# Weight sums for the seven-block back products made inside the second layer, in four of eight slice pairs

## The chip, the cores and the metric

The kernel runs on one core of a Trainium2 chip. The metric is the device time of one execution in microseconds (us), lower being better. A core has TensorE (PE, matmuls), VectorE (DVE), ScalarE (ACT), GpSimd (POOL) and SyncE (SP), which here only issues DMAs. Each engine works off its own queue in order; an instruction at the head of a queue that waits holds back everything behind it.

## What is computed

A circular convolution along the sequence (by FFT), then two gated layers on 6016 tokens with 256 channels. The change is in the second one, `_moe2_ref`.

```python
def reference(**kwargs):
    ...
    attn_out = _attn_ref(**attn_kwargs)      # irfft(rfft(x) * F), (2, 3008, 256)
    x = attn_out.reshape(B * S, D)
    x = _moe_ref(x=x, **moe_kwargs)          # (sigmoid(x @ w_gate) * (x @ w_val)) @ w_out
    return _moe2_ref(x=x, **moe2_kwargs)

def _moe2_ref(x, w_in, w_out):               # w_in (256, 2048), w_out (2048, 256)
    h = x @ w_in
    g = h * (1.0 / (1.0 + np.exp(-1.702 * h)))
    return (g @ w_out).astype(np.float32)
```

## The kernel before

**Numbers.** The weights arrive as 64-bit floats and are decoded on the chip into a high part `hi` and a low part `lo`, both stored as fp32r. A product is three matmuls (`mm3`, lines 126 to 128: hi*hi, hi*lo, lo*hi), here each 128 x 128 weights by 512 tokens (448 in the last round).

**Rounds.** The second layer takes the tokens as six rounds `p` = 0 to 5 of two tiles each (10 tiles of 512, 2 of 448). A round has eight iterations `fp` = 0 to 7, one per pair of 128-wide slices of the 2048 hidden units. An iteration makes the 2 x 2 blocks of hidden values z, y, w, x by seven forward products instead of eight (in program order x0, y4, x5, z1, x6, y2, x3), applies the gate, splits the result into high and low halves, and queues the back products (with `w_out`), which run as `back()` calls between the forward products of the next iteration: one after x0, one after y4, two after z1, two after y2, two after x3.

**Seven-block back products.** An ordinary iteration needs eight back products. In rounds 1 to 5 the iterations with `fp` in `SEVEN = (1, 3, 5)` use seven instead (class `Seven`, `backs()`: m1 to m7). That takes differences of the gate results (t1 to t4: `after_y`, `after_x`, then `third`, `fourth`, `fourth_low` in the next iteration), a bank `ps[3]` shared by m1, m6, m7 and m5, which `keep` (L1847, L1849) empties into `sums` on DVE after each of the four, and four weight sums. One of these sums takes the place of `wp(2 * fp, 1)` in the weight tile itself, three are in `sout` and are reloaded from the DRAM tensor `oscr` for each use (`load_sout`, L1785, L1786).

**Decoding.** The sixteen weight jobs `j` of the second layer (even: `w_in`, odd: `w_out` of slice pair `j // 2`) are decoded by `decode_chores`, a list of small steps that `spend` deals out between the products, from the end of the first layer (L146 loads, L221 to L247 decoding) into round 0. An even job also makes weight sums for the forward products (`sums`, `end`). An odd job of a slice pair in `SEVEN` makes its four back sums in the same steps from the unsplit value, puts the first sum's halves in the `c` buffer, and writes all four to `oscr` (L286, L287). `load_s1` (L1792) brings the first one into the weight tile later in round 0. The `c` buffer is single; L223 of the next job writes it.

**Order.** All engines follow the written order. In round 0, an iteration first runs all steps that its own slice pair still lacks, and only then issues products:

```python
                while 2 * fp + 1 not in done:
                    spend(chores, 1)
```

The same step list carries the splitting of the next round's inputs (`forms_chores`: four differences, then seven high/low splits; L1147, L1152, L1158 to L1170), appended in round 0 at `fp` = 6 at the latest.

Of the kernel before, what the change touches and what calls it, by code (L numbers as in the profile page):

```python
# [89 lines left out]
def kernel(  # L90
# [120 lines left out]
    def decode_chores(j, st, place):  # L211
# [48 lines left out]
        def sums(k):  # L260
# [7 lines left out]
            else:  # L268
                nc.vector.tensor_sub(r[:, 2], v[:, 0, 0], v[:, 0, 1])
                nc.vector.tensor_sub(r[:, 3], v[:, 1, 0], r[:, 1])  # L270
                if j % 2:
                    c = t["c"].bitcast(F32R)
                    t["s1"] = c[:, :P], c[:, P:2 * P]
                else:
                    t["s1"] = hi[:, P:2 * P], lo[:, P:2 * P]
                nc.scalar.activation(out=t["s1"][0], in_=r[:, 0], func=AF.Copy)
                nc.scalar.activation(out=sp[0], in_=r[:, 1:], func=AF.Copy)

        def end():
            r = t["r"]  # L280
# [2 lines left out]
            if j % 2:
                k = SEVEN.index(fp)
                for i in range(2):
                    nc.sync.dma_start(out=oscr[k, i, :, :P], in_=t["s1"][i].bitcast(F32))  # L286
                    nc.sync.dma_start(  # L287
                        out=oscr[k, i, :, P:], in_=sp[i].rearrange("p k m -> p (k m)").bitcast(F32)
                    )
                summed_out.add(fp)  # L290
            else:
                spill()
# [1489 lines left out]
    def load_sout(fp):  # L1782
        k = SEVEN.index(fp)
        for i in range(2):
            nc.sync.dma_start(out=wo[i][:, FC1 - 1, :].bitcast(F32), in_=oscr[k, i, :, P:3 * P])  # L1785
            nc.sync.dma_start(out=sx0[i][:, 5, :].bitcast(F32), in_=oscr[k, i, :, 3 * P:])  # L1786

    def load_s1(fp):
        assert fp in summed_out
        k = SEVEN.index(fp)  # L1790
# [263 lines left out]
```

## Time and profile before

| what | value |
|---|---|
| three timed runs | 1137.73, 1138.62, 1139.47 us (median 1138.62) |
| the profiled execution | 1139.96 us, of which the span is 1138.2 |
| granted TensorE clock, mean of the span | 0.995 |
| busy in the span: PE, DVE, ACT, POOL | 98%, 72%, 59%, 39% |

The span runs from the first to the last instruction; the 1.8 us beside it lie outside the instructions. A matmul's end is modelled, so successive matmuls overlap in the list, and the pitch from start to start tells what one costs. The second layer begins near 647 us: round 0 to 739.5, then five rounds of about 79.6 us (the last one shorter, with 448 tokens a tile).

### The profile page before, as it was taken

To read this page: it belongs to the slowest core of one execution; us is meant where nothing else is said; L and a number is where in the kernel's file an instruction comes from. 1 tells how busy PE (TensorE), PEld (TensorE's weight loads), DVE (VectorE), ACT (ScalarE), POOL (GpSimd) and SP (SyncE) were. 2 spreads that over 40 slices of the span, in tenths; PEclk is the share of its full clock that TensorE was granted. 3 is DMA by queue.
4 is the path that set the end of the run, shared out by engine and by line. 5 is a ranking of instruction groups with operands and counts; after the bars stand their busy time and mean duration, and the time that the engine had idled before them with its cause. 6 is when DMAs were issued, how large, how long until landed. Compare 5 with 4: busy or idle time off the path is not lost.

```text
span 1138.2 us, 15096 instructions
## 1 busy us (share of the span) xinstructions
PE 1119.7 (98%) x5027; PEld 900.1 (79%) x5027; DVE 814.7 (72%) x1369; ACT 668.3 (59%) x1272; POOL 439.6 (39%) x366
## 2 busy tenths in 40 slices
PE   9999999999999999999999998799999999999998
PEld 4378887677888888888888887588888888888897
DVE  6989998786688655878777787747657567477444
ACT  4655555554455545655655656556667657576665
POOL 3810004654333311211211123156566556566554
PEclk9999999999999999999999999899999999999999
DMA  8755238793200300126155262021030020200100
GB/s 203 202 180 181 93 122 224 188 187 81 79 1 1 109 1 1 51 87 131 46 181 186 65 224 75 5 88 29 1 102 15 19 84 15 71 27 15 51 29 32
DMA packets 95244, 99.09 MB, mean 87 GB/s; under 512 B 40320, under 2 KB 67200, under 8 KB 95168
## 3 DMA queue, kind: packets, MB, share of 16 engines
q1 hardware_dynamic: 93200, 95.24, 29.9%
q10 hardware_dynamic: 1968, 2.91, 0.8%
q8 instruction: 39, 0.64, 0.2%
q14 instruction: 37, 0.30, 0.1%
HBM read 61.81 MB, written 32.37 MB: 83 GB/s over the span
## 4 chain that ended last, share of the span: by engine, by line
PE 88%; DVE 4%; DMA 2%; ACT 1%; issue 1%; SPq 0%; POOL 0%; ACTq 0%; DVEq 0%; POOLq 0%
PE ps L126 29%; PE ps L128 29%; PE ps L127 29%; PE ps L344 2%; DVE yp L1152 1%; DMA oscr<-c 0%; DMA wg<-wscr 0%; DMA yraw<-tt 0%; DMA fi<-in_fd_dram 0%; DVE c L235 0%; DVE z L520 0%; DVE a L554 0%; DVE ps L1980 0%; DVE xs L1162 0%; DVE g L1751 0%
## 5 line engine op out<-in xcount | busy, mean ns | idle before, releaser
L1751 POOL TENSOR_TENSOR g<-sg,g 128x512 fp32r<-128x512 f32 (+1 forms) x90 | 122.0, 1360 | 153.1 <-ACT sg L1739 144.7
L123 POOL TENSOR_TENSOR g<-sg,g 128x512 fp32r<-128x512 f32 (+1 forms) x47 | 59.5, 1267 | 257.3 <-ACT g L122 257.3
L126 PE MATMUL ps<-yp,wg 128*128 128x512 f32 (+2 forms) x382 | 149.8, 393 | 0.0
L128 PE MATMUL ps<-yp,wg 128*128 128x512 f32 (+2 forms) x382 | 147.8, 387 | 0.0
L127 PE MATMUL ps<-yp,wg 128*128 128x512 f32 (+2 forms) x382 | 147.7, 387 | 0.0
L127 PE MATMUL ps<-g,wo 128*128 128x512 f32 (+2 forms) x303 | 116.6, 385 | 0.0
L126 PE MATMUL ps<-g,wo 128*128 128x512 f32 (+2 forms) x303 | 116.6, 386 | 0.0
L128 PE MATMUL ps<-g,wo 128*128 128x512 f32 (+2 forms) x303 | 116.5, 385 | 0.0
L1751 POOL TENSOR_TENSOR wo<-sg,wo 128x512 fp32r<-128x512 f32 (+1 forms) x57 | 78.9, 1387 | 53.9 <-ACT sg L1739 48.0
L126 PEld LDWEIGHTS ps<-yp,wg 128*128 128x128 f32 x382 | 71.7, 188 | 26.2 <-issue 13.0
L128 PEld LDWEIGHTS ps<-yp,wg 128*128 128x128 f32 x382 | 71.7, 188 | 14.3
L127 PEld LDWEIGHTS ps<-yp,wg 128*128 128x128 f32 x382 | 71.7, 188 | 13.1 <-issue 0.3
L1966 DVE TENSOR_TENSOR ps<-ps,tabs 128x512 f32<-128x512 f32 (+1 forms) x48 | 32.9, 686 | 61.6 <-PE ps L128 60.4
L1738 ACT ACTIVATE g<-ps 128x512 fp32r<-128x512 f32 (+1 forms) x70 | 41.3, 589 | 58.5 <-DVE ps L1968 55.6
L1649 ACT ACTIVATE sg<-ps 128x480 f32<-128x480 f32 (+1 forms) x48 | 28.1, 586 | 70.4 <-DVE ps L1647 70.4
L1683 DVE TENSOR_TENSOR g<-ps,g 128x480 fp32r<-128x480 f32 (+1 forms) x48 | 32.4, 675 | 48.6 <-ACT g L1680 48.4
L126 PEld LDWEIGHTS ps<-g,wo 128*128 128x128 f32 x303 | 56.9, 188 | 11.5 <-issue 0.8
L128 PEld LDWEIGHTS ps<-g,wo 128*128 128x128 f32 x303 | 56.9, 188 | 10.9
L127 PEld LDWEIGHTS ps<-g,wo 128*128 128x128 f32 x303 | 56.9, 188 | 10.8
L1739 ACT ACTIVATE sg<-ps 128x512 f32<-128x512 f32 (+1 forms) x107 | 62.9, 587 | 0.2 <-POOL g L1751 0.2
L1668 ACT ACTIVATE sg<-ps 128x480 f32<-128x480 f32 (+1 forms) x48 | 28.0, 584 | 39.8 <-PE ps L128 39.6
L1751 POOL TENSOR_TENSOR ks<-sg,ks 128x512 fp32r<-128x512 f32 (+1 forms) x30 | 39.5, 1316 | 28.9 <-ACT sg L1739 24.8
(371 smaller groups left out, 3138.1 us busy)
## 6 DMA issues: line engine op xcount, KB each, us to landing
yscr<-tt SPq DMA_DIRECT2D x56, 128.0 KB, 2.3
raw<-in_w_out_dram SPq DMA_DIRECT2D x14, 512.0 KB, 4.5
yraw<-xscr SPq DMA_DIRECT2D x14, 512.0 KB, 5.1
x<-in_xd_dram SPq DMA_DIRECT2D x32, 192.0 KB, 3.9
wscr<-wl SPq DMA_DIRECT2D x24, 256.0 KB, 2.0
wg<-wscr SPq DMA_DIRECT2D x24, 256.0 KB, 3.0
out_dram<-yraw SPq DMA_DIRECT2D x20, 256.0 KB, 2.2
f<-in_fd_dram SPq DMA_DIRECT2D x23, 192.0 KB, 4.2
```

Source lines behind the costliest of these rows:

```text
L123: lo_eng.tensor_sub(dst_lo, src, dst_hi.bitcast(F32))
L126: nc.tensor.matmul(out=o, lhsT=w[0], rhs=x[0], start=first, stop=False, **kw)
L127: nc.tensor.matmul(out=o, lhsT=w[0], rhs=x[1], start=False, stop=False, **kw)
L128: nc.tensor.matmul(out=o, lhsT=w[1], rhs=x[0], start=False, stop=last, **kw)
L344: nc.tensor.matmul(out=o[c], lhsT=w[64 * r:64 * r + n], rhs=x(r, k), start=True, stop=True, tile_position=(64 * r, 64 * k),)
L1649: nc.scalar.activation(out=sgz, in_=z, func=AF.Sigmoid)
L1668: nc.scalar.activation(out=sgy, in_=y, func=AF.Sigmoid)
L1683: nc.vector.tensor_sub(g0[1], x, g0[0].bitcast(F32))
L1738: nc.scalar.activation(out=self.gp[0], in_=self.bank, func=AF.Gelu_apprx_sigmoid)
L1739: nc.scalar.activation(out=self.sg, in_=self.bank, func=AF.Gelu_apprx_sigmoid)
L1751: eng.tensor_sub(self.gp[1], self.sg, self.gp[0].bitcast(F32))
L1966: nc.vector.tensor_add(y, x, s5[:, :n])
```

## The change

`SEVEN` becomes `(1, 2, 4, 5)`. An odd job's decoding makes no sums any more. New steps `out_sums` add the two halves of the stored weights, make the four sums from that, split them, and write one into the weight tile and three to `oscr`; they are dealt out from the last iteration of round 0 on, into round 1. `load_s1` is gone. In a slice pair that follows another seven-block one, `load_sout` fetches the three parts one at a time, each behind the back product that used it last. m3 goes ahead of m1, the seventh back product goes ahead of `after_x`, and the step rates change.

```diff
-    SEVEN = (1, 3, 5)
-    oscr = dram.tile([len(SEVEN), 2, P, 4 * P], F32, name="oscr")
+    SEVEN = (1, 2, 4, 5)
+    oscr = dram.tile([len(SEVEN), 2, P, 3 * P], F32, name="oscr")
...
-        sums_ = [lambda: sums(0), low, lambda: sums(1), end]
-        if j % 2:
-            sums_ = [low, sums_[0], sums_[2], end] if fp in SEVEN else [low]
-        return [start, mant, sign, value] + sums_
+        return [start, mant, sign, value] + ([low] if j % 2 else [lambda: sums(0), low, lambda: sums(1), end])
...
             if not q and bulk and not hold_back:
                 q.extend(next_decode(bulk.pop(0)))
+            elif not q and out_jobs:
+                q.extend(out_sums(out_jobs.pop(0)))
...
+    def load_sout(fp, *ks):
+        q = SEVEN.index(fp)
+        for k in ks:
+            for i in range(2):
+                nc.sync.dma_start(out=sout[k][i].bitcast(F32), in_=oscr[q, i, :, k * P:(k + 1) * P])
+
+    def out_sums(fp):
+        w = slot(2 * fp + 1)
+        q = SEVEN.index(fp)
+        one, two = ("ex", "c") if q % 2 == 0 else ("c", "ex")
+        t = {}
+
+        def whole():
+            t["v"] = st.tile([P, 512], F32, tag=one, name="wv")
+            nc.vector.tensor_add(t["v"], *[x.bitcast(F32) for x in w])
+
+        def sums():
+            v = t["v"].rearrange("p (c i m) -> p c i m", c=2, m=P)
+            r = t["r"] = st.tile([P, 4, P], F32, tag=two, name="wr")
+            nc.vector.tensor_add(r[:, 0], v[:, 0, 1], v[:, 1, 1])
+            nc.vector.tensor_sub(r[:, 1], r[:, 0], v[:, 0, 0])
+
+        def more():
+            v, r = t["v"].rearrange("p (c i m) -> p c i m", c=2, m=P), t["r"]
+            nc.vector.tensor_sub(r[:, 2], v[:, 0, 0], v[:, 0, 1])
+            nc.vector.tensor_sub(r[:, 3], v[:, 1, 0], r[:, 1])
+            t["hi"] = st.tile([P, 512], F32R, tag="m", name="wh")
+            nc.scalar.activation(out=t["hi"], in_=r.rearrange("p k m -> p (k m)"), func=AF.Copy)
+
+        def low():
+            lo = st.tile([P, 512], F32R, tag=one, name="wlo")
+            nc.vector.tensor_sub(lo, t["r"].rearrange("p k m -> p (k m)"), t["hi"].bitcast(F32))
+            for i, x in enumerate((t["hi"], lo)):
+                nc.sync.dma_start(out=oscr[q, i], in_=x[:, P:].bitcast(F32))
+                nc.sync.dma_start(out=w[i][:, P:2 * P].bitcast(F32), in_=x[:, :P].bitcast(F32))
...
-            return [m1, m3, m6, m2, m7, m4, m5]
+            return [m3, m1, m6, m2, m7, m4, m5]
...
             if p == 0:
+                if fp == LAST:
+                    out_jobs += SEVEN
...
-            if not asked and (fp >= 3 if p else fp >= 4 and not bulk and not chores or fp == 6):
+            if not asked and (fp >= (4 if p == 1 else 2) if p else fp >= 4 and not bulk and not chores or fp == 6):
...
-                rate = (3, 2, 0) if seven else (1, 1, 1) if was else (0, 2, 2) if fp == LAST else (2, 1, 1)
+                if seven:
+                    rate = (1 + (p == 1), 1 + (fp == 2 and p == 1), 0) if was else (3, 2, 0)
+                elif was:
+                    rate = (2, 2, 1) if p == 1 and fp > 3 else (1, 2, 1)
+                else:
+                    rate = (0, 2, 2) if fp == LAST else (2 + (p == 1), 2 + (p == 1), 2)
...
             if seven:
+                back()
                 seven.after_x()
```

Three places show what moves. The first is DVE at the end of round 0. Before, this is the last iteration (`fp` = 7): seven low halves and the last decode (L221 to L247) stand in one block ahead of its first sum (L1966).

```order
L1152 TENSOR_TENSOR xk_1644<-xs,xk_1643 128x512
L221 TENSOR_SCALAR ex<-raw 128x512
L225 TENSOR_SCALAR m<-raw 128x512
L229 SCALAR_TENSOR_TENSOR m<-raw,m 128x512
L235 SCALAR_TENSOR_TENSOR c<-raw,c 128x512
L241 SCALAR_TENSOR_TENSOR m<-m,c 128x512
L247 TENSOR_TENSOR wl_2831<-m,wl_2830 128x512
L1966 TENSOR_TENSOR ps_73<-ps_72,tabs 128x512
```

After, the last decode's final step (L247) stands in `fp` = 5, and the first differences of the next round's inputs follow it there.

```order
L247 TENSOR_TENSOR wl_2831<-m,wl_2830 128x512
L1736 TENSOR_TENSOR g_2871<-ps_73,g_2870 128x512
L1140 TENSOR_TENSOR xs<-yraw 128x512
L1144 TENSOR_TENSOR xs<-yraw,xs 128x512
L1148 TENSOR_TENSOR yraw<-yraw 128x512
L1990 TENSOR_TENSOR ps_73<-ps_71,tabs 128x512
```

The last decode has moved up by two iterations, and no block of steps stands ahead of the first sum of `fp` = 7.

The second place is round 1, iteration `fp` = 1, on DVE in the changed kernel: the sums of the third `out_sums` job (`wr<-wv`) stand between the iteration's second and third sum; the two DMA queues named in the wait are those of the copies that the second job issues from its low half. The SP queue behind them is shown below it, from the last output write (L1757) on.

```order
L1990 TENSOR_TENSOR ps_73<-ps_72,tabs 128x512 [waits PE_49,Activation_49]
L1992 TENSOR_TENSOR ps_71<-ps_71,s_2835 128x512 [waits PE_49]
L1786 TENSOR_TENSOR wr<-wv 128x128 [waits DMAHW4_49,DMAHW3_49,DVE_49]
L1787 TENSOR_TENSOR wr<-wr,wv 128x128 [waits DVE_49]
L1791 TENSOR_TENSOR wr<-wv 128x128
L1792 TENSOR_TENSOR wr<-wv,wr 128x128 [waits DVE_49]
L2006 TENSOR_TENSOR sg<-ps_72,tabs 128x512 [waits PE_49,Pool_49]
```

```order
L1757 DMA out_dram<-yraw 128x512 [waits DMAHW0_49,DVE_49]
L1771 DMA sx_1641<-oscr 128x128 [waits DMAHW1_49]
L1771 DMA sx_1642<-oscr 128x128 [waits DMAHW3_49,DMAHW2_49]
L1771 DMA wo_86<-oscr 128x128
L1771 DMA wo_87<-oscr 128x128 [waits DMAHW4_49]
L1771 DMA wo_86<-oscr 128x128 [waits DMAHW5_49]
L1771 DMA wo_87<-oscr 128x128 [waits DMAHW6_49]
L705 DMA yraw<-xscr 128x2x512 [waits DMAHW7_49]
L705 DMA yraw<-xscr 128x2x512 [waits DMAHW0_49]
L1800 DMA oscr<-wh 128x384 [waits DMAHW1_49]
L1801 DMA wg_84<-wh 128x128 [waits DMAHW2_49,PE_49]
L1800 DMA oscr<-wlo 128x384 [waits DMAHW3_49,DVE_49]
L1801 DMA wg_85<-wlo 128x128 [waits DMAHW4_49,PE_49]
```

Before, nothing stands between those two sums on DVE, and SP has no `oscr` writes in round 1.

The third place is round 2 on DVE, an iteration in which a seven-block pair's back products run. Before (`fp` = 2), from one first sum (L1966) to the next:

```order
L1966 TENSOR_TENSOR ps_73<-ps_71,tabs 128x512
L1968 TENSOR_TENSOR ps_72<-ps_72,s_2835 128x512
L1847 COPY sums<-ps_74 128x512
L1751 TENSOR_TENSOR g_2869<-spare,g_2868 128x512
L1980 TENSOR_TENSOR sg<-ps_71,tabs 128x512
L1847 COPY sums<-ps_74 128x512 x2
L1158 TENSOR_TENSOR xs<-yraw 128x512
L1162 TENSOR_TENSOR xs<-yraw,xs 128x512
L1166 TENSOR_TENSOR yraw<-yraw 128x512
```

After (`fp` = 2, whose own back products are seven too), from the third sum (L2006) on:

```order
L1144 TENSOR_TENSOR xs<-yraw,xs 128x512
L2006 TENSOR_TENSOR sg<-ps_71,tabs 128x512
L1864 COPY sums<-ps_74 128x512
L1823 TENSOR_TENSOR sg<-ps_73,sg 128x512
L1825 TENSOR_TENSOR spare<-sg,ps_73 128x512
L1829 TENSOR_TENSOR sg<-sg 128x512
L1864 COPY sums<-ps_74 128x512
L1736 TENSOR_TENSOR g_2869<-ps_71,g_2868 128x512
L1840 TENSOR_TENSOR spare<-ps_71,sg 128x512
L1148 TENSOR_TENSOR yraw<-yraw 128x512
L1866 TENSOR_TENSOR sums<-sums,ps_74 128x512
```

The differences of `after_y` and `after_x` (L1823 to L1840) now stand among the `keep` copies (L1864, L1866), in one iteration.

## Rows read from the trace of the kernel before

**Rows 1.** Waits of PE's matmuls, longest: engine line, released by, us, times, longest

```profile
PE ps L126 <- ACT s L1946: 8.3, 1, 8.3
PE ps L126 <- DVE wo L1751: 3.2, 1, 3.2
```

**Rows 2.** Windows: stretch, length, busy PE, PEld, DVE, ACT, POOL, clock, DMA, GB/s

```profile
680.00:690.00 10.00, 6.84 (x29) 5.36 (x28) 4.72 (x8) 5.06 (x10) 2.66 (x2) 0.97 0.51 171
690.00:700.00 10.00, 10.00 (x39) 8.12 (x39) 7.84 (x15) 5.70 (x13) 1.29 (x1) 0.86 0.18 60
720.00:730.00 10.00, 1.94 (x9) 1.28 (x7) 9.24 (x16) 4.38 (x9) 0.35 (x1) 0.85 0.00 1
730.00:740.00 10.00, 9.77 (x36) 7.95 (x37) 3.81 (x6) 4.84 (x10) 1.78 (x2) 0.81 0.01 2
...
820.00:900.00 80.00, 80.00 (x355) 66.24 (x354) 50.30 (x73) 53.00 (x99) 48.53 (x36) 1.00 0.13 42
```

**Rows 3.** Chain that ended last, 678 to 688 us: start, us, what

```profile
678.89 5.64 DMA oscr<-c
...
687.34 0.70 DVE wo L1751
```

**Rows 4.** The same chain, 717 to 730 us

```profile
717.16 1.75 DVE xs L1158
...
729.71 0.48 ACT s L1946
```

**Rows 5.** Timeline of PE: start us, us, line, operation, shape; [idle before]

```profile
829.27 0.39 PE L126 MATMUL ps<-sx,wg 128*128 128x512 f32 x1
...
839.47 0.39 PE L126 MATMUL ps<-sx,wg 128*128 128x512 f32 x1
...
1090.03 0.37 PE L126 MATMUL ps<-yp,wo 128*128 128x448 f32 x1
...
1090.64 0.36 PE L126 MATMUL ps<-yp,wo 128*128 128x448 f32 x1
```

**Rows 6.** Timeline of SP's DMA issues at the start of round 1

```profile
748.48 3.25 SPq L1772 DMA_DIRECT2D out_dram<-yraw  x4
751.78 0.43 SPq L1785 DMA_DIRECT2D wo<-oscr  x1
...
753.84 0.89 SPq L723 DMA_DIRECT2D yraw<-xscr  x2
```

**Rows 7.** Landing times of the input loads of line 723, all twelve

```profile
DMA to landing us min/median/max: 4.1/5.1/7.3
```

**Rows 8.** Timeline of DVE: a 128x128 sum, and round 1's third sum

```profile
659.27 0.29 DVE L266 TENSOR_TENSOR wr<-m 128x128 f32<-128x128 f32 x1
...
756.10 0.69 DVE L1980 TENSOR_TENSOR sg<-ps,tabs 128x512 f32<-128x512 f32 x1 [1.41 <-PE ps L128]
```

**Rows 9.** Timeline of DVE in round 2, iterations `fp` = 1 to 4

```profile
835.66 0.69 DVE L1980 TENSOR_TENSOR sg<-ps,tabs 128x512 f32<-128x512 f32 x1 [1.41 <-PE ps L128]
838.33 0.69 DVE L1806 TENSOR_TENSOR sg<-ps,sg 128x512 f32<-128x512 f32 x1 [1.98 <-ACT ps L1742]
...
841.29 0.68 DVE L1823 TENSOR_TENSOR spare<-ps,sg 128x512 f32<-128x512 f32 x1
...
851.13 1.67 DVE L1162 TENSOR_TENSOR xs<-yraw,xs 128x512 f32<-128x512 f32 x1
...
865.35 0.69 DVE L1152 TENSOR_TENSOR yp<-yraw,yp 128x512 fp32r<-128x512 f32 x1
865.96 0.69 DVE L1980 TENSOR_TENSOR sg<-ps,tabs 128x512 f32<-128x512 f32 x1
```

**Rows 10.** Timeline of ACT, then of POOL, behind the same iteration `fp` = 1

```profile
840.58 0.62 ACT L1747 ACTIVATE g<-sg 128x512 fp32r<-128x512 f32 x1
841.10 0.57 ACT L1946 COPY s<-ps 128x512 f32<-128x512 f32 x1
...
839.76 3.06 POOL L1751 TENSOR_TENSOR g<-sg,g 128x512 fp32r<-128x512 f32 x2 [0.65 <-ACT g L1747]
```

More of the change, by code (lines that the diff above doesn't have):

```diff
@@ L270, in sums @@
                 nc.vector.tensor_sub(r[:, 3], v[:, 1, 0], r[:, 1])
-                if j % 2:
[L272 to L276, printed above, removed]
+                nc.scalar.activation(out=hi[:, P:2 * P], in_=r[:, 0], func=AF.Copy)
                 nc.scalar.activation(out=sp[0], in_=r[:, 1:], func=AF.Copy)
@@ L280, in end @@
             r = t["r"]
-            nc.vector.tensor_sub(t["s1"][1], r[:, 0], t["s1"][0].bitcast(F32))
+            nc.vector.tensor_sub(lo[:, P:2 * P], r[:, 0], hi[:, P:2 * P].bitcast(F32))
             nc.vector.tensor_sub(sp[1], r[:, 1:], sp[0].bitcast(F32))
[L283 to L292, printed above, removed]
+            spill()
         low.apart = end.apart = True
-        sums_ = [lambda: sums(0), low, lambda: sums(1), end]
-        if j % 2:
-            sums_ = [low, sums_[0], sums_[2], end] if fp in SEVEN else [low]
-        return [start, mant, sign, value] + sums_
+        return [start, mant, sign, value] + ([low] if j % 2 else [lambda: sums(0), low, lambda: sums(1), end])
     NJ = FC2
@@ L303 @@
     done = set()
-    summed_out = set()
     jobs += [(j, [jobs2[j][0]], jobs2[j][1]) for j in range(EARLY)]
@@ L1197 @@
     bulk = []
+    out_jobs = []
     def chore(q):
@@ L1780, with rest @@
     ]
[L1782 to L1790, printed above, removed]
-        for x, i in zip(wp(2 * fp, 1), range(2)):
-            nc.sync.dma_start(out=x.bitcast(F32), in_=oscr[k, i, :, :P])
+    def load_sout(fp, *ks):
[28 more added lines that the diff above has]
+                nc.sync.dma_start(out=w[i][:, P:2 * P].bitcast(F32), in_=x[:, :P].bitcast(F32))
+        def rest():
+            pass
+        steps = [lambda fn=fn: fn() for fn in (whole, sums, more, low, rest)]
+        for step in steps:
+            step.out = True
+        return steps
     class Seven:
@@ L1849, in keep, with m3 @@
                     nc.vector.tensor_add(dst, dst, self.chain)
+            def m3():
+                mm(c12, sout[2], self.w)
             def m1():
@@ L1853, in m1 @@
                 keep(0)
-            def m3():
-                mm(c12, sout[2], self.w)
             def m6():
@@ L1908 @@
                 hold_back = False
-                while p and chores:
+                while p and chores and not hasattr(chores[0], "out"):
                     chore(chores)
             if p == 0:
+                if fp == LAST:
+                    out_jobs += SEVEN
                 for g in (0, 1, 4, 5, 6, 2, 3):
@@ L1920 @@
                     spend(chores, 1)
-                if fp - 2 in SEVEN:
-                    load_s1(fp - 2)
-            if seven:
-                load_sout(fp)
+            if seven and not was:
+                load_sout(fp, 2, 0, 1)
             lhs = w_parts(fp)
@@ L1954 @@
             queue += held
+            if seven and was:
+                load_sout(fp, 2)
             if fold:
@@ L1973 @@
                 was.fourth_low()
+            if seven and was:
+                load_sout(fp, 0)
             spend(chores, rate[1])
@@ L1990 @@
             if seven:
+                if was:
+                    load_sout(fp, 1)
                 seven.after_y()
@@ L2001 @@
                 bx.low()
-            back()
+                back()
             back()
```

## The prediction

> **What bounds the kernel now.** I read the waits of PE first, then windows of ten microseconds through the second layer, then the chain that ended last where a window shows a loss, then the timelines of DVE, ACT, POOL and SP in a seven-block iteration and at the start of round 1. PE bounds the kernel: in round 2 it is busy for 80.00 of 80 us at full clock [rows 2], and so in rounds 1, 3 and 4. Three matmuls make a product. Iteration `fp` = 1 of round 2 starts at 829.27 and the next at 839.47 [rows 5]: 10.20 us for 45 matmuls, 0.227 us each, 0.68 us a product. At 448 tokens a product is 1090.64 - 1090.03 = 0.61 us [rows 5]. A removed product is therefore time saved, as long as nothing makes PE wait.
>
> PE waits for other engines twice in the second layer, both times in round 0 [rows 1]. I call these A and B.
>
> A: at 685 us, PE is idle for 10 - 6.84 = 3.16 us [rows 2]. The chain shows why: a DMA that carries the first back sum out of the `c` buffer takes 5.64 us, the next decode may not write `c` until it has landed, ACT stands still for that, and the split that PE needs comes at 687.34 [rows 3]. Then PE runs at half clock for a while: the windows at 0.97 and 0.86 [rows 2] give up 0.3 + 1.4 us. A costs 4.9 us.
>
> B: in the last iteration of round 0 all steps that are left are run ahead of the first product. On DVE that block goes from 717.16 to the ACT copy at 729.71 [rows 4]; PE is idle for 8.06 + 0.23 us, and the 0.81 clock of the next window takes 1.9 us more [rows 2] (the 0.85 ahead of it falls into the idle time). B costs 10.2 us.
>
> **What the change takes away.** A goes: no decode writes back sums from `c` any more, so the writer of `c` has no DMA to wait for. B goes: nine decode steps (three for each of three jobs) leave the list, the order shows the last decode ended in `fp` = 5, and the input splits are dealt out over `fp` = 5, 6 and 7. What is left of the splits at the end of round 0 is three DVE operations of 0.69 us, ahead of a first sum that has 3.6 us before its product is ready: covered by the products x0, y4, x5 and two back products. 4.9 + 10.2 = 15.1 us. The bound below is nothing, if another wait takes the place; the bound above is the 15.1, since the rows show no more idle time there.
>
> The fourth seven-block pair takes one product from each of rounds 1 to 5: 4 x 0.68 + 0.61 = 3.3 us. Together 18.4 us.
>
> The decode's removed sums also save DVE time, and fewer sum loads (`load_s1`) save SP issues, in stretches where PE is full: nothing. The order m3 before m1 costs nothing: the POOL operation that makes m3's low half is the second of its iteration, over a microsecond before the iteration ends. The DMAs of the three parts of `sout` go from four to six per use; they are issued seven microseconds and more ahead of the product that needs them, against a queue that stands idle for most of a round (0.13 DMA share [rows 2]): nothing, and at most their 0.4 us of issue time.
>
> **What it adds, first part: a DVE wait in round 1.** I call this C. In `fp` = 1 of round 1, the third `out_sums` job wants to write the buffer from which the second job's low half is copied out. Those copies stand on SP behind four output writes, six `sout` loads and two input loads. The output writes end at 748.48 + 3.25 = 751.73, and four `sout` loads and the input loads begin at 751.78 and 753.84 [rows 6]. With two more `sout` loads and some delay of the evacuations by the new ACT steps, the input loads go out at 754.8 to 756.5, and the four copies by 757.1 to 758.2. Input loads land 5.1 us after issue [rows 7], and copies that were issued behind such loads waited for them in A (5.64 us [rows 3]). So the buffer comes free at 759.5 to 761.5. Behind the waiting operation on DVE stand three more small sums (4 x 0.29 in all [rows 8]) and then the third sum of the iteration, which is due at 756.10 [rows 8]; it comes at 760.6 to 762.6. Product x3 has to wait until that sum has read its bank. PE gets there at 749.67 + 12 x 0.68 = 757.8, and is let through at 761.3 to 763.4: 3.5 to 5.6 us of idle time. A's 3.16 us of idle time were followed by 1.7 us of lost clock, so 0 to 1.7 more. I take 5.5 us: near the lower half, since all but one of these steps are sums of durations that could overlap better than I add them. If SP or the loads are much earlier than I think, C is nothing; the far end is 7.5.
>
> **Second part: two seven-block pairs in a row.** I call this D; the trace has no such place, so it is put together from a seven-block iteration and the one behind it. Times are from the start of the first one, 829.27. The third sum comes at 835.66 and the first difference at 838.33, 9.06 after the start [rows 9]; the third high part at 840.58, and the next iteration's copy of x0 ends at 841.67, 12.40 after the start [rows 10]. Product x5 of that next iteration needs this copy; it is due four products into it, at 10.20 + 2.72 = 12.92. In a pair the second iteration starts at 7 + 7 products, 14 x 0.68 = 9.52, so x5 is due at 12.24 and comes some 0.25 us late. The same holds for the low half that m6 needs: POOL ends its second split at 839.76 + 3.06 = 842.82 [rows 10], 13.55 after the start, and m6 is due at 9.52 + 4.08 = 13.60. So every microsecond by which the differences come late is now lost on PE, where 0.7 us of slack stood before. Ten such places (two in each of five rounds) cost 2.7 us if nothing else comes late.
>
> DVE makes things late. In the middle iteration it has 13 operations of its own, 13 x 0.60 = 7.8 us by their pitch, and one or two steps, in 9.52 us. A step ahead of the third sum makes that sum late: at 865.35 a split, and the third sum at 865.96 [rows 9], where 859.19 + 6.39 = 865.58 was due: 0.38. Six places in rounds 2 to 4 have one such step (2.3 us), round 1 has the four operations of a job (1.0). A step between the last difference and the first `keep` of the next iteration delays m6, which waits for the bank: 0.35 to 0.45 in five places (1.8), and as much in the first iteration of the pair in four places (1.6; the last difference ends at 841.97 there [rows 9], so there is less to lose). Round 5 has no steps. D: 2.7 + 2.3 + 1.0 + 1.8 + 1.6 = 9.4 us, about 0.9 a pair. Below, D is nothing, if the engines have more room than I see; a wait on DVE can't make PE faster, so there is no gain. Above, see the first rival.
>
> **The sum.** Against the profiled execution of 1139.96 us: 1139.96 - 15.1 - 3.3 + 5.5 + 9.4 = 1136.5. That execution is 1.3 us above the median of the timed runs, so against the median 1138.62 it is 1135.1.
>
> **Rivals.** R1, slower: D costs 2 us a pair. The place is DVE in the middle iterations of rounds 1 to 4, the price is a step of 1.67 us, as at 851.13, in place of the 0.69 of 865.35 [rows 9]. Some 18 steps stand in the path; if about ten take 1.0 us more, D is 20 and the time is 1138.6 - 18.4 + 5.5 + 20 = 1145.7. It decides from D = 12.9, that is 1.3 a pair. For it: POOL is busy for most of the stretch behind the differences [rows 10], and these steps read and write SBUF. Against: the step at 865.35 kept its 0.69 right beside a POOL operation.
>
> On that, the Trainium skill (SBUF — State Buffer, Who interferes with whom) says that a DVE instruction with two SBUF inputs and a GpSimd one that reads SBUF exclude each other for the whole instruction, whoever starts first. By this rule every step that begins under a POOL split loses up to that split's remainder, and R1 is the rule's outcome if most of them begin there. The two rows above fit it, one from either side; how often each happens in a pair no row shows, and I give it the chance below.
>
> R2, much faster: C is hidden (the copies land before 756) and the pairs have only the 0.25 us: 1138.6 - 18.4 + 2.7 = 1122.9. For it: DVE's idle time of 28% over the span, and C rests on one chain of SP issues. Against: SP's order at that place is plain, and the input loads are as large as those in A.
>
> R3, the change does not do what it says in round 0: some other wait, as for a reload or a raw weight load, takes the place of A or B, half of the 15.1 us stays, and the time is 1142.7. For it: the DMAs of round 0 are still many. Against: the decode ends two iterations ahead of its use.
>
> **How the numbers follow.** Forecast 0.54, R1 0.19, R2 0.17, R3 0.10. A measurement of this kernel tells about 0.2%, 2.3 us, from no change: the band is 1136.3 to 1140.9. Within the forecast's own case (1130 to 1141) I put 0.32 faster, 0.19 same, 0.03 slower; R2 is faster; R1 is slower but for 0.02; R3 is 0.02 faster, 0.03 same, 0.05 slower. That gives faster 0.51, same 0.24, slower 0.25. The range 1124 to 1146 leaves out about 0.1 on either side; the likeliest case's own is 1130 to 1141.
>
> **What would show it.** Right: round 0 without a PE wait and at clock 1.00 from 650 to 730; in round 1, `fp` = 1, a DVE wait of 4 to 6 us on a copy out of `wlo`, with PE waiting for the third sum (L2006); in rounds 2 to 4, PE waits of a few tenths at x5, z1 or m6 behind each pair, none in round 5 beyond 0.3; rounds 2 to 4 about 1 to 2 us longer than 79.6 - 0.7. Wrong: any PE wait of microseconds in round 0, no DMA wait on DVE in round 1, or rounds 2 to 4 shorter than 79.2 us (D is small) or longer than 83 (R1).

## The result and the profile after

The changed kernel takes 1147.96 us (median of 4, 1147.61 to 1148.03) against 1138.55: 1.0082 times the time of before, 95% interval 1.0064 to 1.0099. It is 9.4 us slower; 3.5 us faster was forecast, and the range ended at 1146.0. The profiled execution spans 1146.0 us, the one of before 1138.2.

PE's waits, from the waits of its matmuls (engine and line, released by, us, times, longest). The two of [rows 1] are gone, and four groups stand in their place:

```profile
PE ps L126 <- DVE sg L2006: 7.8, 2, 7.0
PE ps L126 <- DVE sums L1866: 5.3, 9, 1.5
PE ps L126 <- DVE sums L1864: 2.4, 7, 0.4
PE ps L126 <- ACT s L1968: 1.7, 1, 1.7
```

L2006 is the third sum (L1980 of before), L1864 and L1866 are `keep`, L1968 is the copy of x0. The windows, with the columns of [rows 2]:

```profile
680.00:690.00 10.00, 10.00 (x46) 8.29 (x45) 8.84 (x14) 6.37 (x13) 3.00 (x2) 1.00 0.20 76
690.00:700.00 10.00, 10.00 (x46) 8.29 (x45) 9.62 (x16) 6.99 (x15) 2.62 (x2) 1.00 0.01 2
720.00:730.00 10.00, 10.00 (x46) 8.26 (x45) 8.81 (x16) 6.98 (x13) 2.78 (x2) 1.00 0.06 22
730.00:740.00 10.00, 8.33 (x37) 6.59 (x36) 7.20 (x12) 5.78 (x11) 5.42 (x4) 1.00 0.39 137
740.00:750.00 10.00, 3.91 (x18) 2.90 (x16) 1.33 (x5) 1.09 (x2) 1.29 (x1) 0.95 0.68 198
750.00:760.00 10.00, 9.12 (x30) 7.33 (x31) 7.10 (x12) 6.68 (x12) 5.84 (x4) 0.70 0.15 50
760.00:770.00 10.00, 8.64 (x36) 6.03 (x35) 8.51 (x14) 5.72 (x11) 5.30 (x4) 1.00 0.15 43
820.00:900.00 80.00, 78.37 (x342) 63.41 (x341) 57.71 (x84) 52.95 (x99) 50.48 (x36) 1.00 0.15 47
```

Round 0, where A and B stood, is full at clock 1.00. The losses are in round 1, from 736 us on, and smaller ones in every later round. The table gives each round's length, from one ACT copy of x0 in iteration 0 to the next round's (in the changed kernel L1968, at 643.75, 724.35, 821.06, 902.86, 984.68 and 1066.16). The three columns on the right are kernels of the next section.

| round | before | changed | copies on ACT's queue | three pairs, placed | four pairs, placed |
|---|---|---|---|---|---|
| 0 | 95.49 | 80.60 | 80.62 | 80.63 | 80.63 |
| 1 | 79.50 | 96.71 | 87.96 | 81.01 | 87.31 |
| 2 | 79.56 | 81.80 | 81.83 | 79.31 | 78.75 |
| 3 | 79.56 | 81.81 | 81.83 | 79.56 | 79.51 |
| 4 | 79.49 | 81.49 | 81.48 | 79.49 | 79.50 |
| 5, 7 iterations | 62.68 | 62.81 | 62.93 | 62.78 | 63.21 |

So round 0 gives 14.9 us and round 1 takes 17.2. To see what takes them I added up, in PE's timeline, by how much the distance from one matmul's start to the next exceeds 0.227 us. That counts the wait, the 0.11 us by which the first matmul behind a wait is longer, and the half clock. Round 1 has 17.5 us of it in four pieces:

- E, 1.9 us at 736: PE waits for ACT's copy of x0. It was not forecast.
- C, 9.6 us at 743: 7.1 of waiting and 2.5 of half clock, until 756.
- 4.0 us at 763 to 773, in the iterations with the back products of the first two pairs.
- 2.0 us at 792 to 805, the same for the other two.

Rounds 2, 3 and 4 have 2.5 to 2.7 us each. Round 5, where matmuls are 0.203 us apart, has 0.7.

C and E, in DVE's timeline (start, us; in brackets the idle time ahead and what ended it):

```profile
732.39 1.27 DVE L1786 TENSOR_TENSOR wr<-wv 128x128 f32<-128x128 f32 x1
733.69 1.43 DVE L1787 TENSOR_TENSOR wr<-wr,wv 128x128 f32<-128x128 f32 x1
...
749.20 0.29 DVE L1786 TENSOR_TENSOR wr<-wv 128x128 f32<-128x128 f32 x1 [8.64 <-DMA wg<-wlo]
...
750.14 0.68 DVE L2006 TENSOR_TENSOR sg<-ps,tabs 128x512 f32<-128x512 f32 x1
```

POOL's splits beside the first two of these rows:

```profile
732.21 1.30 POOL L1736 TENSOR_TENSOR wo<-sg,wo 128x512 fp32r<-128x512 f32 x1 [0.89 <-ACT sg L1724]
733.67 1.30 POOL L1736 TENSOR_TENSOR ks<-sg,ks 128x512 fp32r<-128x512 f32 x1 [0.17 <-DVE wr L1786]
```

SP's issues, ACT's copies and the landing of the DMA that DVE waits for (from the chain of work that ended last):

```profile
732.63 5.83 SPq L1757 DMA_DIRECT2D out_dram<-yraw  x4
...
741.46 0.95 SPq L705 DMA_DIRECT2D yraw<-xscr  x2
...
744.27 0.55 SPq L1801 DMA_DIRECT2D wg<-wlo  x1
```

```profile
735.55 0.63 ACT L1794 ACTIVATE wh<-wr 128x512 fp32r<-128x512 f32 x1 [1.96 <-DVE wr L1792]
...
737.51 0.61 ACT L1968 COPY s<-ps 128x512 f32<-128x512 f32 x1
```

```profile
744.27 4.81 DMA wg<-wlo
```

The wait C is where it was forecast, on the DMA that was named, with the third sum late behind it and PE idle for 6.97 us. E stands ahead of it: two of the second job's small sums take 1.27 and 1.43 us in place of 0.29, so ACT's `wh` waits 1.96 us for them, and the evacuations and the copy of x0 queue behind it.

In rounds 2 to 4 the waits are for `keep`, four a round. Two of them are m6's, which waits for the `keep` behind m1. Round 2, DVE, then POOL, then PE:

```profile
843.01 1.48 DVE L1140 TENSOR_TENSOR xs<-yraw 128x512 f32<-128x512 f32 x1
844.41 0.68 DVE L1864 COPY sums<-ps 128x512 f32<-128x512 f32 x1
...
854.39 1.23 DVE L1148 TENSOR_TENSOR yraw<-yraw 128x512 f32<-128x512 f32 x1
855.55 0.68 DVE L1866 TENSOR_TENSOR sums<-sums,ps 128x512 f32<-128x512 f32 x1
```

```profile
840.88 3.06 POOL L1736 TENSOR_TENSOR g<-sg,g 128x512 fp32r<-128x512 f32 x2 [0.65 <-ACT g L1732]
...
852.03 3.04 POOL L1736 TENSOR_TENSOR wo<-sg,wo 128x512 fp32r<-128x512 f32 x2 [0.66 <-ACT wo L1732]
```

```profile
845.14 0.50 PE L126 MATMUL ps<-g,wo 128*128 128x512 f32 x1 [0.32 <-DVE sums L1864]
...
856.28 0.50 PE L126 MATMUL ps<-wo 128*128 128x512 f32 x1 [0.60 <-DVE sums L1866]
```

The step L1140 starts under a POOL split that ends at 843.94 and ends itself at 844.49, 0.55 us later; L1148 ends at 855.62, 0.55 us behind the POOL work that ends at 855.07. The `keep` behind each is late by that.

The other two are waits of the next m1 for the `keep` behind m5, which stands behind the three differences. A step ahead of the third sum makes that sum late, and with it the differences. Round 2, DVE, then PE:

```profile
847.40 0.68 DVE L1144 TENSOR_TENSOR xs<-yraw,xs 128x512 f32<-128x512 f32 x1
848.01 0.68 DVE L2006 TENSOR_TENSOR sg<-ps,tabs 128x512 f32<-128x512 f32 x1
...
852.60 0.68 DVE L1864 COPY sums<-ps 128x512 f32<-128x512 f32 x1
```

```profile
853.33 0.50 PE L126 MATMUL ps<-ks,wg 128*128 128x512 f32 x1 [0.36 <-DVE sums L1864]
```

With the longer matmul behind each, m6's waits are 0.5 to 0.6 and 0.8 to 0.9 us, m1's 0.6 to 0.7. In round 1 the longest of the short waits, 1.5 us, is m6's too: two small sums of the fourth job start under POOL splits ahead of its `keep` (DVE):

```profile
770.18 0.83 DVE L1791 TENSOR_TENSOR wr<-wv 128x128 f32<-128x128 f32 x1
770.94 1.36 DVE L1792 TENSOR_TENSOR wr<-wv,wr 128x128 f32<-128x128 f32 x1
772.22 0.68 DVE L1866 TENSOR_TENSOR sums<-sums,ps 128x512 f32<-128x512 f32 x1
```

### The profile page after: what moved, and what is told of

It reads as the page before. It is cut to its first block, busy times and chain, and to the rows that moved or that the text cites. A ratio compares the mean times of both kernels' runs of the same rounds, so it can differ in the third digit from the quotient of the medians.

```text
span 1146.0 us, 15293 instructions
## 1 busy us (share of the span) xinstructions
PE 1121.4 (98%) x5012; PEld 893.5 (78%) x5012; DVE 850.6 (74%) x1425; ACT 677.8 (59%) x1285; POOL 454.9 (40%) x371
## 4 chain that ended last, share of the span: by engine, by line
PE 78%; DVE 10%; ACT 3%; DMA 2%; issue 2%; SPq 1%; POOL 0%; DVEq 0%; POOLq 0%; ACTq 0%
PE ps L126 26%; PE ps L127 25%; PE ps L128 25%; PE ps L326 1%; DVE sums L1866 1%; ACT sg L1724 1%; DVE sg L1823 1%; DVE sg L2006 1%; ACT ps L1727 1%; DVE sums L1864 1%; DVE sg L1829 1%; DMA x<-in_xd_dram 1%; DVE spare L1825 1%; DVE ps L1990 1%; DVE spare L1840 0%
## 5 line engine op out<-in xcount | busy, mean ns | idle before, releaser
L1736 POOL TENSOR_TENSOR g<-sg,g 128x512 fp32r<-128x512 f32 (+1 forms) x89 | 125.0, 1408 | 136.3 <-ACT sg L1724 107.9
L123 POOL TENSOR_TENSOR g<-sg,g 128x512 fp32r<-128x512 f32 (+1 forms) x47 | 59.6, 1267 | 257.1 <-ACT g L122 257.1
L126 PE MATMUL ps<-g,wo 128*128 128x512 f32 (+2 forms) x309 | 119.5, 388 | 3.2 <-DVE sums L1866 2.5
L127 PE MATMUL ps<-g,wo 128*128 128x512 f32 (+2 forms) x309 | 119.0, 386 | 0.0
L128 PE MATMUL ps<-g,wo 128*128 128x512 f32 (+2 forms) x309 | 118.9, 386 | 0.0
L1736 POOL TENSOR_TENSOR wo<-sg,wo 128x512 fp32r<-128x512 f32 (+1 forms) x61 | 82.6, 1358 | 63.2 <-ACT sg L1724 59.3
L126 PEld LDWEIGHTS ps<-g,wo 128*128 128x128 f32 x309 | 58.0, 188 | 16.9 <-DVE sums L1866 3.8
L1634 ACT ACTIVATE sg<-ps 128x480 f32<-128x480 f32 (+1 forms) x48 | 28.1, 586 | 71.0 <-DVE ps L1632 71.0
L128 PEld LDWEIGHTS ps<-g,wo 128*128 128x128 f32 x309 | 58.0, 188 | 11.1
L127 PEld LDWEIGHTS ps<-g,wo 128*128 128x128 f32 x309 | 58.0, 188 | 10.9
L1723 ACT ACTIVATE g<-ps 128x512 fp32r<-128x512 f32 (+1 forms) x63 | 37.3, 592 | 44.2 <-DVE ps L1992 42.3
L1724 ACT ACTIVATE sg<-ps 128x512 f32<-128x512 f32 (+1 forms) x97 | 57.1, 589 | 0.2 <-POOL g L1736 0.2
L1866 DVE TENSOR_TENSOR sums<-sums,ps 128x512 f32<-128x512 f32 (+1 forms) x60 | 40.2, 669 | 17.1 <-PE ps L128 17.1
L126 PE MATMUL ps<-yp,sx 128*128 128x512 f32 (+2 forms) x129 | 50.0, 387 | 0.1
```

The costliest lines, as they stand in the source:

```text
L123: lo_eng.tensor_sub(dst_lo, src, dst_hi.bitcast(F32))
L126: nc.tensor.matmul(out=o, lhsT=w[0], rhs=x[0], start=first, stop=False, **kw)
L127: nc.tensor.matmul(out=o, lhsT=w[0], rhs=x[1], start=False, stop=False, **kw)
L128: nc.tensor.matmul(out=o, lhsT=w[1], rhs=x[0], start=False, stop=last, **kw)
L1634: nc.scalar.activation(out=sgz, in_=z, func=AF.Sigmoid)
L1723: nc.scalar.activation(out=self.gp[0], in_=self.bank, func=AF.Gelu_apprx_sigmoid)
```

## The experiments

Times of before beside the three groups of runs below: 1139.02, 1138.83 and 1139.39 us.

**1. Copies from ACT's queue.** In `low()` of the jobs, four DMAs a job:

```
-                nc.sync.dma_start(out=oscr[q, i], in_=x[:, P:].bitcast(F32))
-                nc.sync.dma_start(out=w[i][:, P:2 * P].bitcast(F32), in_=x[:, :P].bitcast(F32))
+                nc.scalar.dma_start(out=oscr[q, i], in_=x[:, P:].bitcast(F32))
+                nc.scalar.dma_start(out=w[i][:, P:2 * P].bitcast(F32), in_=x[:, :P].bitcast(F32))
```

> The changed kernel, but the sixteen copies of the four jobs' halves (four per job) are issued from ACT's queue instead of SP's, so they no longer stand behind the output writes, the sout loads and the input loads. Theory C (the third job's write on DVE waits for the second job's copies because these stand late in SP's queue): the 8.6 us DVE wait at 749 us of the changed kernel's trace goes, and with it 7.1 us of PE pitch and 2.5 us of half clock behind it, 9.6 us together: 1138.4 us; if the 3.8 us of short PE waits at 763 to 773 us were its backlog, down to 1134.6. Rival 1 (the jobs' own steps on DVE and ACT, and not the queue, are the price; the wait only hides them): at most 3 us come back, 1145 or more. Rival 2 (issuing from ACT delays the evacuations there by 0.5 us a copy): 1140 to 1142.

Measured: 1139.87 us, ratio to before 1.0010 (0.9998 to 1.0022). The third job's first small sum waits for nothing (DVE's timeline):

```profile
739.75 0.28 DVE L1786 TENSOR_TENSOR wr<-wv 128x128 f32<-128x128 f32 x1
```

8.1 us of the median come back (8.8 in round 1 by the table), and no half clock is left there. So C's price was the queue in which the copies stood. Rival 1 is out. The waits at 763 to 773 stay, 10 us earlier: they were not C's backlog. (C's own 9.6 us did not come back whole, since a new wait of 0.6 us stands at 749.)

**2. Three pairs, none in a row.**

```
-    SEVEN = (1, 2, 4, 5)
+    SEVEN = (1, 3, 5)
```

> The changed kernel with seven-block pairs at iterations 1, 3 and 5 (three instead of four, so no two in a row); the weight sums are still made by the new jobs. Theory D (two pairs in a row cost, by DVE's keep copies coming late): the PE waits of rounds 2 to 5, 2.7 us in each of rounds 2 to 4 and 0.6 in round 5, go, and some 4 to 6 us of round 1's; 3.3 us of products come back; the wait C of round 1 and the 1.9 us ahead of it stay: 1136 to 1139 us. Rival (the short waits come from the forms' steps on DVE beside POOL wherever a pair stands, and not from two in a row): three places stay where four were, 1147 to 1151.

Measured: 1145.76 us, ratio 1.0056 (1.0034 to 1.0078). Neither theory: only 2.2 us, where I expected nine or more. Round 0 is 80.65, so A and B go with the sums' move alone, without the fourth pair. C is still there. Rounds 2 to 4 still lose 1.8 us each, though no pair follows another, and round 1 has a new wait of 2.0 us behind two long steps:

```profile
776.84 1.47 DVE L1140 TENSOR_TENSOR xs<-yraw 128x512 f32<-128x512 f32 x1
778.33 1.65 DVE L1144 TENSOR_TENSOR xs<-yraw,xs 128x512 f32<-128x512 f32 x1
779.90 0.67 DVE L1866 TENSOR_TENSOR sums<-sums,ps 128x512 f32<-128x512 f32 x1
```

So most of D is not the price of two pairs in a row, but of the changed table of rates and the earlier start of the forms, which put steps where POOL splits.

**3. Steps out of the second pair.** Rounds 2 to 5 run none in a pair's second iteration, and none in the first slot of the iteration behind it:

```
-                    rate = (1 + (p == 1), 1 + (fp == 2 and p == 1), 0) if was else (3, 2, 0)
+                    rate = (1 + (p == 1), 1 + (fp == 2 and p == 1), 0) if was and p == 1 else (0, 0, 0) if was else (3, 2, 0)
...
-                    rate = (2, 2, 1) if p == 1 and fp > 3 else (1, 2, 1)
+                    rate = (2, 2, 1) if p == 1 and fp > 3 else (1, 2, 1) if p == 1 else (0, 2, 2)
```

> The changed kernel, but in rounds 2 to 5 no step of the next round's forms is run in an iteration that is the second pair of two in a row, and in the iteration behind it the first slot is empty too; the steps are run later. Theory D1 (the keep copies come late because a step stands ahead of them, lengthened from 0.69 to 1.2 or 1.5 us beside a POOL split): of the 2.7 us in each of rounds 2 to 4, the two waits behind such a step go, 1.5 us a round, or all of it but the wait behind the differences: 1142 to 1144 us. Rival D2 (DVE's own thirteen operations don't fit into an iteration of fourteen products, steps or no steps): 1146.5 to 1148.5. If the steps that are moved crowd the end of the round: 1149 or more.

Measured: 1145.03 us, ratio 1.0049 (1.0031 to 1.0067); 1.0 us a round come back, less than the 1.5 of D1. What was left is a new wait, since I had put two steps ahead of a third sum, and the second started under a POOL split (DVE, then POOL, then PE):

```profile
857.44 1.67 DVE L1144 TENSOR_TENSOR xs<-yraw,xs 128x512 f32<-128x512 f32 x1
859.03 0.68 DVE L2006 TENSOR_TENSOR sg<-ps,tabs 128x512 f32<-128x512 f32 x1
```

```profile
856.72 1.84 POOL L1736 TENSOR_TENSOR ks<-sg,ks 128x512 fp32r<-128x512 f32 x1 [1.27 <-ACT sg L1724]
```

```profile
859.76 0.50 PE L126 MATMUL ps<-sx,wg 128*128 128x512 f32 x1 [0.89 <-DVE sg L2006]
```

Two waits of 0.18 us a round stay at the `keep` behind the differences, for which m1 waits, 0.29 with the longer matmul behind each: the bare price of a pair in a row.

**4. Third job later.** SP's order as it is; in iteration 1 of round 1 two steps instead of five:

```
-                    rate = (1 + (p == 1), 1 + (fp == 2 and p == 1), 0) if was else (3, 2, 0)
+                    rate = (1 + (p == 1), 1 + (fp == 2 and p == 1), 0) if was else (2, 0, 0) if p == 1 and fp == 1 else (3, 2, 0)
```

> The changed kernel with SP's order as it is, but in round 1 the third job starts an iteration later (two steps are run in iteration 1 instead of four), so that its first write to the buffer comes after the second job's copies have landed. Theory C: the 9.6 us of the wait go, and one or two come back where the job's steps now stand in the pairs' iterations: 1138.4 to 1140.5 us. Rival (the jobs' steps are the price wherever they stand): 1145 or more, with new PE waits of several us in iterations 2 and 3 of round 1.

Measured: 1141.88 us, ratio 1.0021 (1.0010 to 1.0031). C is gone without any change on SP, as the theory has it, and 6.1 us come back; the job's first steps, now at 748.10 (1.47 us) and 749.61 (1.24), stand ahead of a `keep` and cost 2.1 us and some half clock. The number misses the expectation by 1.4, for the same reason as in 2 and 3.

**5 to 7. Steps dealt out anew**, on top of the copies on ACT's queue. Experiment 5 changes round 1 alone, 6 rounds 2 to 5 alone (the forms are also asked an iteration later), 7 both; the last is

```
+                rate = (((3, 3, 0), (3, 2, 0), (0, 0, 0), (0, 1, 4), (3, 2, 0), (0, 0, 0), (0, 1, 3), (2, 3, 3))
+                        if p == 1 else
+                        ((0, 0, 0), (0, 0, 0), (0, 0, 0), (0, 1, 2), (3, 2, 0), (0, 0, 0), (0, 2, 2), (0, 2, 2)))[fp]
```

> The kernel of the run with the copies on ACT's queue (1139.87 us), with the steps of round 1 alone dealt out anew: none in the last slot of iteration 0, none in iterations 2 and 5, the third and the fourth job in iterations 3 and 4, the forms in 4, 6 and 7. Theory: what is left of round 1's loss (8.9 us in that run: 2.0 us where PE waits for ACT behind stretched 128x128 sums of the second job, 4.3 us in iterations 1 to 3 and 2.5 us in iterations 4 to 6) comes from where the steps stand, and about 6 us of it go: 1133 to 1135 us. Rival (the jobs' and forms' steps are too many for round 1 wherever they stand): 1138 or more.

> The kernel with the copies on ACT's queue (1139.87 us), with the steps of rounds 2 to 5 alone dealt out anew: none in iterations 2 and 5, none in the first slot of iterations 3 and 6 and one, not two, ahead of the third sum of iteration 3. Theory (a step costs only where it stands ahead of a keep or a third sum and starts beside a POOL split): of the 2.9 us lost in each of rounds 2 to 4, 0.6 us stay, the bare price of two pairs in a row: 1133 us. Rival (the pairs themselves cost it): 1138 or more.

> Both of the last two edits on top of the copies on ACT's queue. If they add up: 1139.87 - 6 - 6.9 = 1127 us, which is what the products saved and the two stalls of round 0 are worth (1138.6 - 18.4 = 1120.2) and some 6 us of waits that stay. If one gives back what the other gains: 1133 or more.

Measured: 1136.99 us (0.9984, 0.9974 to 0.9994), 1133.52 (0.9954, 0.9938 to 0.9970) and 1131.23 (0.9932, 0.9917 to 0.9947). Number 6 is the theory's 1133: no wait is left in rounds 2 to 4 but the bare 0.29 of each pair. In 5 and 7 round 1 loses E and most of the short waits and gets a new one: ACT holds its next evacuation until it has issued the DMA of a low half that DVE has not finished (ACT, then PE):

```profile
767.54 0.47 ACTq L1801 DMA_DIRECT2D wg<-wlo  x1
768.06 0.60 ACT L1723 ACTIVATE wo<-ps 128x512 fp32r<-128x512 f32 x1 [2.59 <-DVE wv L1781]
```

```profile
769.68 0.80 PE L126 MATMUL ps<-yp,wo 128*128 128x512 f32 x1 [2.58 <-ACT s L1965]
```

That and the half clock behind it cost 4.4 us in 7 and 4.7 in 5: the price of a queue that shares its engine with the evacuations.

**8. POOL's splits out.** On top of 1, and so for `t2` and `t3`:

```
-            self.t1.low()
+            if now[0] < 2:
+                self.t1.low()
```

> The kernel with the copies on ACT's queue (1139.87 us); in rounds 2 to 5 three low halves of each seven-block pair, those of t1, t2 and t3, are left out on POOL (the products read old values), the steps stand where they stood. Theory (a DVE operation with both inputs in SBUF waits for a running POOL split): the steps take 0.69 us again, the waits for keep behind them go, 0.6 us of the 2.9 us a round stay: 1133 us. Rival (DVE has too many operations there, whatever POOL does): 1138 or more, the steps ahead of the late keep copies at 0.69 us and the waits as long as before.

Measured: 1136.75 us, ratio 0.9980 (0.9967 to 0.9993). The same two steps as at 843.01 and 854.39 above:

```profile
836.42 0.68 DVE L1140 TENSOR_TENSOR xs<-yraw 128x512 f32<-128x512 f32 x1
...
847.22 0.68 DVE L1148 TENSOR_TENSOR yraw<-yraw 128x512 f32<-128x512 f32 x1
```

1.48 and 1.23 us become 0.68: POOL is what made them long. But of the 2.8 us a round only 1.1 go, not 2.3: a step of 0.69 us makes a `keep` late too, most of all by way of the third sum and the differences. Of the m6 waits one goes and the other falls from 0.9 to 0.3 us; those of m1 stay at 0.7. With experiment 6 this divides rounds 2 to 4: 1.1 us a round for the lengthening, 1.1 for the steps at their normal length, 0.6 for the two bare pairs.

**9. Only the table**, copies back on SP; rounds 2 to 5 as in 7.

```
-        steps = [lambda fn=fn: fn() for fn in (whole, sums, more, low, rest)]
+        steps = [lambda fn=fn: fn() for fn in (whole, sums, more, low)]
...
+                rate = (((3, 2, 0), (3, 1, 0), (0, 0, 0), (0, 1, 4), (3, 2, 0), (0, 0, 0), (0, 2, 2), (0, 3, 4))
+                        if p == 1 else
```

> The changed kernel with its copies on SP as they are, and only the table of steps dealt out anew: in round 1 the third and fourth jobs in iterations 3 and 4, no steps in the iterations that are the second of two pairs, the forms behind them; in rounds 2 to 5 as in the run with those rounds' steps dealt out anew. (The job's empty fifth step is dropped.) Theory: 1131.23 less the 4.7 us that run lost at the end of iteration 3 of round 1, where ACT's queue waited for a low half before issuing its copy, less about 1 us of waits in iteration 7: 1125 to 1127 us. Rival (on SP the copies stand behind the loads again and the wait C comes back in another iteration): 1133 or more.

Measured: 1131.53 us, ratio 0.9927 (0.9912 to 0.9942). The later rounds are as hoped. Round 1 is not: two jobs stand one behind the other at the start of iteration 4, and the first sum there comes late; that is its one long wait:

```profile
PE ps L126 <- DVE ps L1984: 3.9, 1, 3.9
```

Neither the theory's number nor the rival's place: SP's copies make DVE wait for 0.6 us ahead of that sum, and the jobs' own steps are the rest.

**10. `keep` ahead of the difference**, on top of 9:

```
         def after_y(self):
...
-            nc.vector.tensor_sub(w.sg, w.sg, z.sg)
-            self.t2.sg = w.sg
...
         def after_x(self):
+            x, z, w = self.x, self.z, self.w
+            nc.vector.tensor_sub(w.sg, w.sg, z.sg)
+            self.t2.sg = w.sg
```

> The same kernel, and the last difference of after_y (t2's, on DVE) is made behind the keep that stands after it. Theory (the 0.3 us that every second pair in a row still costs are the 0.3 us by which this keep comes late behind the difference): 3 us less than the run without it, 1122 to 1124 us. Rival (t2's low half on POOL then comes late for the product m6): no gain, or up to 3 us slower, 1125 to 1130.

Measured: 1142.69 us, ratio 1.0027 (1.0017 to 1.0037), 11 us slower than 9. The rival's sign, not its place or size: the difference now starts under a POOL split and takes 1.47 us, ACT's `t2.high()` waits for it, and the copy of x0 stands behind that on ACT. PE waits ten times for that copy:

```profile
PE ps L126 <- ACT s L1962: 10.7, 10, 1.1
```

**11. Three pairs, placed.** Pairs at 1, 3 and 5, the sums in jobs, copies on SP, the forms' steps in rounds 2 to 5 as in the kernel before:

```
+    SEVEN = (1, 3, 5)
+                rate = (((3, 1, 0), (3, 1, 0), (0, 0, 0), (3, 1, 0), (1, 1, 1), (3, 2, 0), (1, 1, 1), (0, 2, 3))
+                        if p == 1 else
+                        ((0, 0, 0), (0, 0, 0), (0, 0, 0), (3, 2, 0), (1, 1, 1), (3, 2, 0), (1, 1, 1), (0, 2, 2)))[fp]
```

> Three seven-block pairs at iterations 1, 3 and 5, the sums made by the new jobs, steps placed so that none stands where PE waited. It measures what the fourth pair is worth when nothing else is in the way. Theory: the fourth pair saves 3.3 us of products and costs 0.3 us at each of ten places where two follow each other, 0.3 us net: within 1 us of the kernel with four pairs, 1125 to 1128 us. Rival 1 (two in a row cost nothing once the steps are placed): 3.3 us slower than it, 1129. Rival 2 (they cost more than they save): 1123 or less.

Measured: 1125.72 us (1125.06 to 1126.85), ratio to before 0.9878 (0.9861 to 0.9895): the fastest kernel of the study, 13.7 us ahead of before and 22 ahead of the change. From the second layer's start on, the waits of PE that the view lists come to 0.6 us (first row), and round 2 is full again (windows):

```profile
PE ps L126 <- DVE sums L1863: 0.6, 2, 0.3
```

```profile
820.00:900.00 80.00, 80.00 (x355) 66.24 (x354) 51.14 (x75) 52.69 (x98) 48.19 (x35) 1.00 0.13 43
```

What the fourth pair is worth is read from round 3, which no stall of round 1 reaches: 79.51 us with four pairs placed, 79.56 with three. It saves 0.68 and costs 2 x 0.29. As whole kernels the three pairs are 5.8 us ahead of number 9, by rival 2's sign, but that is number 9's stall in round 1 (87.31 against 81.01), not a price of the pairs. Four pairs without that stall were not run.

## Why the prediction was wrong

What failed are three terms of the sum. C's copy was taken to land too early (5.5 us taken, 9.6 measured). The small sums of the jobs were priced at 0.29 us wherever they stand, so that E stood at nothing (1.9 measured). And D's steps were priced at their normal length, where POOL splits made many of them longer (9.4 taken, 14.7 measured).

**A and B: right.** 15.1 us were to go from round 0; 14.9 went (95.49 to 80.60), and nothing took their place. Experiments 2 and 11 show that the sums' move does it, with three pairs as well as four. R3 is out. The steps costed at nothing (m3 ahead of m1, two more `sout` loads a pair, fewer DMAs in the decode) cost nothing that PE waited for.

**The products: right**, 0.68 us each.

**C: right in place and cause, too small.** 5.5 was taken, 7.5 was the far end, 9.6 it was. The step that failed is the time at which the copy lands. I let the copies land when the input loads ahead of them do, 5.1 us after those were issued, that is 2.4 to 3.3 us after the end of the copies' own issue. It was 4.26 from there (4.81 from the start of the issue), and the row that said so stood in the prediction: 5.64 us for a copy behind such loads [rows 3]. The lost clock was 2.5, not at most 1.7. The SP part of the sum was near where nothing disturbed it: number 9's second job issues its last copy at 742.99, 8.8 us after its iteration starts at 734.18, and 7.4 to 8.5 was worked out. In the changed kernel it is 744.82 - 733.62 = 11.2 us, since E makes the output writes late: 5.83 us from the first to the last, 3.25 before [rows 6]. Less the 1.9 us by which E holds PE itself, the buffer comes free 13.5 us after the iteration's start, where 9.8 to 11.8 was worked out: the landing makes 1.0 to 1.9 of the difference, SP's lateness about as much.

**E: missed.** The four small sums were priced at 0.29 each by [rows 8]. Two of them started under POOL splits and took 1.27 and 1.43.

**D: the bare pair right in size but not in place, the steps too small.** 0.25 us a pair was put on x0's copy on ACT, though the two times beside it, 12.40 and 12.24, differ by 0.16, and on POOL's low half for m6. 0.29 was measured, in experiments 3, 6 and 9, and 0.36 in round 5, which has no steps; but there it is m1 that waits, for the `keep` behind the differences on DVE. That the sizes agree is luck. Experiment 10 shows that x0's copy comes next: with this `keep` moved ahead, PE waits for the copy.

What the steps add was put at 6.7 us in rounds 1 to 4. In rounds 2 to 4 alone it was 6.2 (8.0 us, less six places at 0.29), and that the two numbers are near each other is luck. The steps ahead of third sums were priced well: 0.38 each, and m1's waits are 0.3 to 0.4 above the bare 0.29 in six places. m6's waits were priced too low: 0.35 to 0.45 each by steps of 0.69, and 0.5 to 0.9 measured behind steps of 1.2 to 1.5. In round 1 the short waits were 4.0 + 2.0 us, where the sum had about 2: there small sums and steps of the forms stand under POOL splits. With round 5's 0.7, D is 14.7, not 9.4.

**The sum** by measured terms: -14.9 - 3.3 + 1.9 + 9.6 + 14.7 = +8.0 us. Against the forecast, C was 4.1 too small, D 5.3, E 1.9, and A and B brought 0.2 less: 11.5 us, which is the way from the -3.5 forecast to these +8.0. By the table the second layer got 8.9 us longer, so 0.9 lies in differences too small for the terms. The two profiled spans differ by only 7.8, as the second layer happened to begin 1.2 us earlier in the changed kernel's execution (first copy of x0 at 643.75 against 644.95; the other kernels' lie between 642.95 and 645.35). The timed medians differ by 9.4.

**R1 was the case that came**, with D above its 12.9. That its 1145.7 us lie near the 1147.96 is partly luck: D was 14.7 and not its 20, and C and E were 6.0 us more than its sum had. Its mechanism is shown by experiment 8, in which the lengthening is worth 1.1 us a round. The argument that I held against it was a misreading: the step at 865.35 that kept its 0.69 [rows 9] was not under a POOL operation. POOL began 0.07 us after it and was itself the one that waited (the trace of before, POOL):

```profile
865.42 1.77 POOL L1751 TENSOR_TENSOR g<-sg,g 128x512 fp32r<-128x512 f32 x1 [1.59 <-ACT sg L1739]
```

Starts had to be compared, not the fact that two rows lie beside each other. Counted over rounds 2 to 4 of before, from the timelines of DVE and POOL, the answer was there to be read: of the 512-wide DVE operations with both inputs in SBUF, all 8 that started under a running POOL operation took 1.25 us or more, and all 32 others 0.69 or less.

R2's hidden C did not come about, but its other half did, in number 9's later rounds: pairs with nothing but 0.29 us each.

## What to carry to other kernels

When steps are moved to other places, price each one by what the neighbouring engines run at its new place: a subtraction that costs 0.29 or 0.69 us alone cost 1.2 to 1.7 here under a split, and its place ahead of an operation that PE waits for decides whether that counts. A copy behind large loads on a queue is priced by the row of such a copy, from its own issue. And a change made of two parts is worth trying apart: the move of the sums is worth 13.7 us once its steps are placed, and the fourth pair, for which they were moved, nothing that shows.

## What the runs showed of the hardware

In rounds 2 to 4 of the changed kernel, every 512-wide DVE operation with two SBUF inputs that started while a POOL operation ran (8 of 8) ended 0.55 us after that operation's end, however much of it was left, and took 1.23 to 1.78 us; the 38 that started clear of POOL took 0.67 to 0.69, and so did 136 that had one input in PSUM and started under POOL (0.67 to 0.70). It holds the other way round for POOL: 1.77 us in place of 1.30 behind a DVE operation that began first. The Trainium skill (SBUF — State Buffer, Who interferes with whom) says that a DVE instruction with two SBUF inputs and a GpSimd one that reads SBUF get in each other's way, and that one with a single SBUF input does not; the trace agrees, with the numbers above.

A wait of PE costs more than its length: the first matmul behind each short wait is followed at 0.34 us and not at 0.227, so the 0.18 us of the bare pair cost 0.29. Behind the wait of 7.1 us, ten matmuls followed at 0.43 us, the lower of the two clock levels; behind the wait E none did in experiment 1 (1.9 us) and eight did in experiment 8 (2.1 us).
